# A first sweep whose engine order is worked out in the source: wide ranks, turned tails, decay of two pairs on TensorE

## The chip, the cores and the metric

The kernel runs on one core of one Trainium2 chip. The metric is the device time of the whole program in microseconds (us), as the median of several executions; one execution was also taken by the hardware profiler, and all rows below come from that one.

## The reference

Eight batches of 576 tokens go through eight attention heads of width 64, then a low-rank mixing over tokens, then a two-layer dense net.

```python
scores = q @ k.T / 8                     # per batch and head, 576 x 576
cum    = cumsum(log(clip(f, 1e-4, 1)))   # decay along the sequence
scores = where(causal, -1e9, scores + cum[:, None] - cum[None, :])
x      = softmax(scores) @ v             # heads side by side: 576 x 512
u      = x + ((x.T @ U) @ V).T           # U 576 x 32, V 32 x 576
out    = u + relu(u @ w1) @ w2           # w1 512 x 2048, w2 2048 x 512
```

All is float32. The term `cum[:, None]` is the same along a row and drops out of the softmax.

## The kernel before

Products are done on TensorE in a one-pass format (`F32R`) with each operand split in a high and a low part, three matmuls for one product (high x high, low x high, high x low). The first six pairs of heads use plain float32 scores instead (`terms`, line 291).

**Three stages.** The *first sweep* goes over 32 pairs of heads (four pairs to a batch). For each pair it does attention; for each batch it then does the ranks (`x.T @ U`), the mixing, and the first 6 of 16 chunks of the hidden width of the dense net. It writes `u` and the partial sums to device memory (`ud`, `accd`). A *hand-over* (from line 887) mixes the last batch and does its share of the dense net, while the weights of the other ten chunks are loaded and decoded. The *second sweep* (from line 1075) does those ten chunks for all batches; the change leaves it alone but for the name of one tile.

**A pair of heads.** The 576 rows are four row blocks of 128 and a tail of 64. The scores of a row block i for both heads (`score`, line 297) are matmuls on 64 rows of the array each, into two PSUM banks; `run_a` does blocks 3, 1 and 0, `run_b` block 2 and the tail. For each block, VectorE adds the masked decay and takes the maximum (line 315), and ScalarE takes the exponential (line 324). `turn_p` (line 395) transposes the result on TensorE into a T bank, from where ScalarE or VectorE copies it to `PT` (lines 389, 391). `turn_tail` and `turn_keys` do it for the tail: the last one transposes 64 columns alone (128 x 64). `values` (line 436) multiplies with v, `turn_x` (line 453) transposes back and scales with the reciprocal sums from `inverse` (line 378), `turn_last` does so for the tail, again as a transpose of 64 columns. `split_x` (line 471) makes the high and low parts, and `ranks` (line 485) multiplies them with U, once for each pair, 128 columns wide.

**Decay and masks.** The cumulated decay of all heads is worked out once, written to `cumd` in device memory (line 684) and loaded back for each pair, broadcast over the partitions (`load_decay`, `load_tail`, two buffers each). GpSimd makes the masks from it (`mask`, line 156). Pair 0 doesn't wait for that: TensorE adds its decay with a second matmul, whose weights `picks` hold -8 in the row of the pair's head (line 307).

**Weights.** 14 pieces of the weights (`UNITS`) are loaded as 64-bit numbers and decoded to float32 by six steps (`decode_steps`, line 58): one on ScalarE, four of VectorE's instructions (lines 75, 76, 79, 80), an addition on GpSimd (line 84), a cast on ScalarE (line 85) and a subtraction on GpSimd (line 86). All 14 are decoded within the first seven pairs.

**Dense work.** `ffn_units` (line 577) lists the dense work of a batch as units: six for the first layer of each group of tokens (`l1`, twelve matmuls, tile `A`) and three for each tile of 128 tokens of the second layer (`l2`, six matmuls each, tile `B`). An even batch has 24 units, an odd one 27.

**The order.** `step(t)` (line 720) writes out one pair in ten slots by hand: what TensorE does in each slot, what is put off by how many slots (`defer`), which masks, loads and decodes go where. Dense units are filled in at some slots; `HELD = 4` units of a batch stay over. In the first five steps there is no dense work, and a matmul on `busy` stands in most slots to keep TensorE active (`stay_awake`, line 650). In those steps all engines run in the order of the source (`manual_schedule(engines=None)`); later TensorE, the DMA queue (SP) and GpSimd do, while the compiler's scheduler orders VectorE and ScalarE.

```python
with tc.manual_schedule(engines=None):
    for t in range(EARLY):
        step(t)
with tc.manual_schedule(engines={ET.PE, ET.SP, ET.Pool}):
    for t in range(EARLY, LAST + 1):
        step(t)
```

PSUM has eight banks: four for scores (S), two for transposes and values (T), two for mixing and dense work (F).

Of the kernel before, what the change touches and what calls it, by code (L numbers as in the profile page):

```python
# [8 lines left out]
F32 = mybir.dt.float32  # L9
# [10 lines left out]
DM = H * D  # L20
# [17 lines left out]
NF = 6  # L38


@with_exitstack
def tile_decay_attention_moe(ctx, tc, qk, v, f, U, V, w1, w2, out):
# [56 lines left out]
    sf2 = pool("sf2", 2)  # L99
# [5 lines left out]
    sb2 = pool("sb2", 2)  # L105
    sb3 = pool("sb3", 3)
    psF = ctx.enter_context(tc.tile_pool(name="psF", bufs=2, space=PSUM))
    psS = banks.enter_context(tc.tile_pool(name="psS", bufs=4, space=PSUM))
    psT = banks.enter_context(tc.tile_pool(name="psT", bufs=2, space=PSUM))
# [6 lines left out]
    warm = att.tile([P, 512], BF16, name="warm")  # L116
# [4 lines left out]
    for vr in VR:  # L121
        nc.gpsimd.memset(vr[64:128, NM], 0.0)
    PT4 = att.tile([P, P], F32, name="PT4")
    nc.gpsimd.memset(PT4[64:128], 0.0)
# [3 lines left out]

    def load_decay(p):
        if p >= NP:  # L130
            return
        z = st.setdefault(p, {"M": {}})
        z["decay"] = sb2.tile([P, 2, MAIN], F32, tag="decay", name=f"decay{p}")
        m = z["M"][NM] = sb2.tile([P, S], F32, tag="Mt", name=f"M{p}_t")
        if p == 0:
            nc.gpsimd.memset(z["decay"], 0.0)
            nc.gpsimd.memset(m, 0.0)
            return
        src = cumd.rearrange("(j p) s -> p j s", j=2)[p, :, 0:MAIN]
        nc.sync.dma_start(z["decay"], src.unsqueeze(0).broadcast_to([P, 2, MAIN]))  # L140

    def load_tail(p):
        if not 0 < p < NP:
            return
        m = st[p]["M"][NM]
        for j in range(2):
            nc.sync.dma_start(m[OWN[j]], cumd[j * B * NHP + p].unsqueeze(0).broadcast_to([64, S]))

    def mask(p, i):
        if p >= NP:  # L150
            return
        z = st[p]
        if i < NM:
            w = P * (i + 1)
            m = z["M"][i] = sb.tile([P, 2, w], F32, tag=f"M{i}", name=f"M{p}_{i}")
            nc.gpsimd.affine_select(  # L156
                m, z["decay"][:, :, 0:w], [[0, 2], [-1, w]], ALU.is_ge, MASKED, base=P * i, channel_multiplier=1
            )
            return
        for j in range(2):  # L160
            d = z["M"][NM][OWN[j], MAIN:S]
            nc.gpsimd.affine_select(d, d, [[-1, TAIL]], ALU.is_ge, MASKED, base=0, channel_multiplier=1)
# [24 lines left out]
    staged = {}  # L187

    def load_w(u):
        if u in staged or u >= len(UNITS):  # L190
            return
        kind, fc = UNITS[u]
        n = {"U": (NM + 1) * RK, "V": S}.get(kind, 512)
        if kind == "w2":

            spare = xn[NX - 1].rearrange("p c d -> p (c d)").bitcast(I32)
            if fc % 2:
                raw, a = spare[:, 1536:2560], sb.tile([P, 512], I32, tag="w2a", name=f"stg{u}")
            else:
                raw, a = spare[:, 0:1024], spare[:, 1024:1536]  # L200
        else:
            t = sf.tile([P, 3 * S], I32, tag=("uh", "ul", "hh", "hl")[u % 4], name=f"stg{u}")
            raw, a = t[:, 0 : 2 * n], t[:, 2 * n : 3 * n]
        staged[u] = raw.rearrange("p (n t) -> p n t", t=2), a
        if kind == "w1":
            nc.sync.dma_start(raw, w1_src(fc))
        elif kind == "w2":
            nc.sync.dma_start(raw, w2_src(fc))
        elif kind == "V":
            for g in range(4):  # L210
                nc.sync.dma_start(raw[32 * g : 32 * g + 32], words(V))
        else:
            r4 = raw.rearrange("p (c r) -> p c r", c=NM + 1)
            nc.sync.dma_start(r4[:, 0:NM], words(U[0:MAIN]).rearrange("(c p) r -> p c r", p=P))
            for g in range(2):
                nc.sync.dma_start(r4[64 * g : 64 * g + 64, NM], words(U[MAIN:S]))

    def decode_w(u, spread=None):
        load_w(u)
        raw, a = staged.pop(u)  # L220
        staged[u] = None
        kind, fc = UNITS[u]
        if kind == "w1":
            h, l = (x[:, fc].rearrange("p c f -> p (c f)") for x in (w1h, w1l))
        elif kind == "w2":
            h, l = w2h[:, fc], w2l[:, fc]
        elif kind == "V":
            h, l = VV, VV
        else:
            raw = raw.rearrange("p (c r) t -> p c r t", c=NM + 1)  # L230
            a = a.rearrange("p (c r) -> p c r", c=NM + 1)
            h, l = Us[:, :, 0:RK], Us[:, :, RK : 2 * RK]
        steps = decode_steps(raw, a, h, l, nc.scalar, slice(96, 128) if kind == "V" else slice(0, 128), keep=spread is None)
        if spread:
            for fn, (slots, phase) in zip(steps, spread):
                if slots:
                    defer(phase, fn, slots)
                else:
                    fn()
            return  # L240
        for fn in steps:
            fn()
        if u == len(UNITS) - 1:
            nc.gpsimd.memset(xn[NX - 1][64:128, NM, :], 0.0)


    st = {}
    filler = []

    later = {}  # L250
    now = [0]

    def defer(phase, fn, slots=1):
        later.setdefault(now[0] + slots, []).append((phase, fn))

    def run_later():
        now[0] += 1
        for _, fn in sorted(later.pop(now[0], []), key=lambda x: x[0]):
            fn()

    def run_filler():
        w, fn = filler.pop(0)
        fn()
        return w

    def load_qk(p):

        if p >= NP:
            return
        b, hp = divmod(p, NHP)  # L270
        raw = RAW[p % 2]
        st.setdefault(p, {"M": {}}).update(b=b, hp=hp, raw=raw)
        nc.sync.dma_start(raw[:, KO:QW], qk[p, :, 1])
        nc.sync.dma_start(raw[:, 0:MAIN], qk[p, :, 0, 0:MAIN])
        for j in range(2):
            nc.sync.dma_start(raw[OWN[j], QT + 64 * j : QT + 64 * j + 64], qk[p, OWN[j], 0, MAIN:S])

    def split_qk(p):
        z = st[p]
        z["hi"] = sb.tile([P, QW], F32R, tag="qkh", name=f"qkh{p}")  # L280
        z["lo"] = sb.tile([P, QW], F32R, tag="qkl", name=f"qkl{p}")
        split(z["hi"], z["lo"], z["raw"], nc.scalar, nc.gpsimd)

    def load_v(p):

        vr = VR[p % 2]
        st[p]["vr"] = vr.rearrange("p c (j d) -> p c j d", j=2)
        nc.sync.dma_start(vr[:, 0:NM], v[p, 0:MAIN].rearrange("(c p) d -> p c d", p=P))
        nc.sync.dma_start(vr[0:64, NM], v[p, MAIN:S])

    def terms(p):
        z = st[p]
        if p < NF:
            return ((z["raw"], z["raw"]),)
        return ((z["hi"], z["hi"]), (z["lo"], z["hi"]), (z["hi"], z["lo"]))
# [1197 lines left out]
```

## Time and profile before

| | |
|---|---|
| median of 3 executions | 1247.96 us (1247.14 to 1250.01) |
| the profiled execution, own time | 1248.86 us |
| its span, first to last instruction | 1247.1 us |
| mean granted clock of TensorE | 0.98 |
| the last matmul of the sweep's last ranks | 724.7 us of the span |
| the hand-over ends, second sweep begins | 776.8 us |

The time of an execution is the span and 1.8 us around it. PE is TensorE's matmul unit, PEld its weight loads (beside the matmuls), DVE VectorE, ACT ScalarE, POOL GpSimd, SP the engine whose queue issues nearly all DMAs. Matmuls are pipelined: the row of a matmul shows how long it was under way, so what one costs in a sequence is the distance between starts. A granted clock of 1.00 is TensorE's full level (2.4 GHz), 0.5 its lower one (1.2 GHz).

### The profile page before, as it was taken

The page shows a single profiled execution, that of the slowest core. Times are in us where ns is not written, and L with a number is a line of the kernel's source. Part 1 is how long each engine was busy: PE and PEld are TensorE (multiplying, and loading weights), DVE is VectorE, ACT ScalarE, POOL GpSimd, SP SyncE. Part 2 cuts the span into 40 slices and gives each one's busy share as a digit, 9 for nine tenths or more (in the row PEclk, how much of TensorE's full clock was granted, in tenths as well). Part 3 has the DMA queues.
Part 4 walks back from the last instruction along what each step waited for, and adds up shares of the span by engine and source line. Part 5 has one row for each costly group of instructions (what it writes and reads, how often), then busy time and mean ns, then how long its engine had stood idle before and what let it go on. Part 6 is the DMA issues. An engine that isn't in the chain of part 4 may idle for free.

```text
span 1247.1 us, 23786 instructions
## 1 busy us (share of the span) xinstructions
PE 1178.3 (94%) x8484; PEld 1007.9 (81%) x8489; DVE 841.9 (68%) x2151; ACT 638.2 (51%) x1675; POOL 300.4 (24%) x420
## 2 busy tenths in 40 slices
PE   7777799999999999999998999999999999999998
PEld 4445677886786886878777888878899999999998
DVE  6668856556556556556557679858778687786765
ACT  4565455554555545546536433344555655555553
POOL 4654744333343423434324100000000000000000
PEclk8998899999999999999999999999999999999999
DMA  7544432543535425336325355965775664745533
GB/s 216 152 143 132 126 108 77 163 107 84 150 101 171 120 58 180 103 76 186 109 68 176 119 186 171 336 209 190 236 234 165 208 203 159 256 159 189 191 113 105
DMA packets 124984, 194.36 MB, mean 156 GB/s; under 512 B 16001, under 2 KB 58241, under 8 KB 122817
## 3 DMA queue, kind: packets, MB, share of 16 engines
q1 hardware_dynamic: 124592, 192.57, 49.8%
q8 instruction: 67, 1.10, 0.4%
q14 instruction: 53, 0.43, 0.1%
q10 hardware_dynamic: 272, 0.26, 0.1%
HBM read 145.46 MB, written 47.33 MB: 155 GB/s over the span
## 4 chain that ended last, share of the span: by engine, by line
PE 77%; DVE 10%; issue 3%; DMA 3%; ACT 3%; POOL 3%; SPq 0%; POOLq 0%; ACTq 0%; DVEq 0%
PE pf L1133 15%; PE A L599 12%; PE B L617 10%; PE po L1225 8%; PE V L445 6%; PE T L404 4%; PE px L1225 4%; PE pf L1225 2%; PE Hb L956 2%; PE S_0c L303 2%; PE po L1240 2%; PE O L972 2%; DVE PT L391 2%; PE S_0b L303 1%; PE S_0t L351 1%
## 5 line engine op out<-in xcount | busy, mean ns | idle before, releaser
L1356 ACT COPY mc<-pf 128x512 f32<-128x512 f32 x139 | 81.6, 587 | 168.8 <-PE pf L1133 168.8
L1284 POOL TENSOR_TENSOR xn<-xn,xn 128x512 f32<-128x512 f32 x1 | 1.3, 1267 | 529.5 <-DMA out_dram<-xn 529.5
L404 PE MATMUL T<-ident,P 128*128 128x128 f32 x640 | 103.0, 282 | 24.7 <-ACT PT L389 8.8
L156 POOL TENSOR_SCALAR_AFFINE_SELECT M<-decay 128x1024 f32<-128x1024 f32 (+3 forms) x128 | 94.9, 761 | 119.4 <-DVE nm L315 89.2
L599 PE MATMUL A<-uh,w1h 128*128 128x256 f32 (+1 forms) x384 | 120.8, 315 | 1.0 <-DVE hl L603 0.6
L599 PE MATMUL A<-ul,w1h 128*128 128x256 f32 (+1 forms) x384 | 114.2, 297 | 0.0
L404 PEld LDWEIGHTS T<-ident,P 128*128 128x128 f32 x640 | 77.1, 144 | 45.6 <-ACT PT L389 11.1
L599 PE MATMUL A<-uh,w1l 128*128 128x256 f32 (+1 forms) x384 | 113.9, 297 | 0.0
L176 POOL TENSOR_TENSOR qkl<-raw,qkh 128x1216 fp32r<-128x1216 f32 x26 | 73.1, 2813 | 167.6 <-ACT qkh L173 150.7
L391 DVE COPY PT<-T 128x256 f32<-128x256 f32 (+1 forms) x192 | 73.4, 417 | 44.4 <-PE T L404 43.9
L617 PE MATMUL B<-w2h,hh 128*128 128x512 f32 x216 | 91.4, 423 | 3.4 <-DVE ost L631 3.4
L445 PE MATMUL V<-PT,vr 128*64 128x448 f32 (+3 forms) x640 | 92.0, 435 | 1.5 <-ACT PT L389 1.5
L617 PE MATMUL B<-w2l,hh 128*128 128x512 f32 x216 | 85.1, 394 | 0.0
L617 PE MATMUL B<-w2h,hl 128*128 128x512 f32 x216 | 84.8, 393 | 0.0
L607 ACT ACTIVATE hh<-A 128x256 fp32r<-128x256 f32 (+1 forms) x96 | 39.6, 413 | 86.5 <-PE A L599 86.4
L445 PEld LDWEIGHTS V<-PT,vr 128*64 128x64 f32 x640 | 41.7, 139 | 48.4 <-issue 35.3
L599 PEld LDWEIGHTS A<-uh,w1h 128*128 128x128 f32 x384 | 73.2, 191 | 3.4 <-DVE hl L603 0.8
L603 DVE SCALAR_TENSOR_TENSOR hl<-A,hh 128x256 fp32r<-128x256 f32 (+1 forms) x96 | 43.3, 451 | 45.1 <-ACT hh L607 45.0
L599 PEld LDWEIGHTS A<-uh,w1l 128*128 128x128 f32 x384 | 73.5, 191 | 0.1
L599 PEld LDWEIGHTS A<-ul,w1h 128*128 128x128 f32 x384 | 73.2, 191 | 0.1
L1133 PE MATMUL pf<-d,b1h 128*128 128x256 f32 x320 | 69.6, 280 | 1.3 <-DVE fd L961 1.3
L1137 DVE TENSOR_TENSOR fd<-xn,fd 128x256 fp32r<-128x256 f32 x70 | 38.9, 556 | 34.6 <-ACT fd L1177 32.1
(329 smaller groups left out, 3819.7 us busy)
## 6 DMA issues: line engine op xcount, KB each, us to landing
un<-ud SPq DMA_DIRECT2D x16, 1024.0 KB, 6.4
decay<-cumd SPq DMA_DIRECT2D x31, 512.0 KB, 6.4
d<-ud SPq DMA_DIRECT2D x48, 256.0 KB, 3.8
twd<-xn SPq DMA_DIRECT2D x40, 256.0 KB, 2.9
raw<-in_qk_dram SPq DMA_DIRECT2D x32, 288.0 KB, 6.4
Th<-twd SPq DMA_DIRECT2D x35, 256.0 KB, 3.6
tw<-twd SPq DMA_DIRECT2D x35, 256.0 KB, 2.8
Tl<-twd SPq DMA_DIRECT2D x35, 256.0 KB, 3.2
```

What stands on the lines that cost most here:

```text
L156: nc.gpsimd.affine_select(m, z["decay"][:, :, 0:w], [[0, 2], [-1, w]], ALU.is_ge, MASKED, base=P * i, channel_multiplier=1)
L176: leng.tensor_tensor(dl, src, dh.bitcast(F32), op=ALU.subtract)
L391: defer(2, lambda: nc.vector.tensor_copy(dst, src))
L404: nc.tensor.transpose(tp[:, P * (x + c) : P * (x + c) + P], z["P"][j][i][:, P * c : P * c + P], ident)
L445: nc.tensor.matmul(ps, vr[:, c, j], pt[:, j, c, lo:hi], start=c == 0, stop=lo == 0)
L599: nc.tensor.matmul(ps[:, :nt], wt[:, fc, c], ut[:, c, sl], start=m == 0, stop=m == 3 * NDC - 1)
L603: nc.vector.scalar_tensor_tensor(hl[:, fc, :nt], ps[:, :nt], 0.0, hh.bitcast(F32)[:, fc, :nt], op0=ALU.max, op1=ALU.subtract)
L607: defer(3, lambda: nc.scalar.activation(hh[:, fc, :nt], ps[:, :nt], AF.Relu))
L617: nc.tensor.matmul(ps, ht[:, fc, P * x : P * x + P], wt[:, fc], start=fc == 0 and m == 0, stop=fc == NA - 1 and m == 2,)
L1133: nc.tensor.matmul(ps, a[x][:, c], b[y][:, c], start=start and m == 0, stop=m == 5, skip_group_check=True)
L1225: nc.tensor.matmul(ps[:, HT * x : HT * x + HT], f[a][:, P * x : P * x + P], w[b], start=k.i == 0 and m == 0 and x == 0 and not (k.n == NG ...
L1356: nc.scalar.copy(mc, FA)
```

## The change

All of the first sweep is now described as operations, each with what it reads and writes (keys), its engine or engines with a planned duration, a rank `pr`, and the PSUM banks that it opens and uses. `run()` takes them one after the other: for each engine it finds the operations whose inputs are there (by planned times), takes among those that could start first the one of the lowest rank, and of the engines the one that starts earliest. That gives an order for all five engines, which is then fixed.

```diff
+TURN = 0.08
+AHD = 1.2
+LATE = 2.5
+DEEP = 3.0
+DUE = [0.3, 0.9, 1.5, 2.1, 2.7, 3.3, 3.9, 4.4, 4.8, 5.0, 5.2, 5.5, 5.8, 6.1]
...
+    HOMES = {"S": (0, 1, 2, 3), "T": (4, 5), "F": (6, 7)}
+    LAG = {"PE": 0.23, "DVE": 0.17, "ACT": 0.17, "POOL": 0.12, "SP": 0.06}
+    SLACK = {"PE": 0.25, "DVE": 0.1, "ACT": 0.1, "POOL": 0.1, "SP": 0.0}
...
+    def copy(n, dst, src):
+        return [("ACT", 0.133 + 0.00068 * n, lambda: nc.scalar.copy(dst(), src())), ("DVE", 0.064 + 0.00104 * n, lambda: nc.vector.tensor_copy(dst(), src()))]
+
+    def load(pr, nbytes, fn, r=(), w=()):
+        return op([("SP", 0.45, fn)], pr, r, w, lands=nbytes / 200e3)
...
+    def run():
...
+                        est = max(now, o.ready)
...
+                            if kind == "T" and not state["dense"]:
+                                allowed = (4, 5, 7)
...
+                        if e == "SP":
+                            est = max(est, state["pipe"] - DEEP)
+                        if e == "PE" and o.mode != state["mode"]:
+                            est += 0.15
+                            pr += TURN
+                        cand.append((est, pr, o.n, o, dur, fn, homes))
...
+                first = max(now, min(c[0] for c in cand)) + SLACK[e]
+                c = min((c for c in cand if c[0] <= first), key=lambda c: (c[1], c[2]))
+                if best is None or c[0] < best[0]:
+                    best = (c[0], e, c)
...
+            if e == "PE":
+                if not state["dense"]:
+                    for _ in range(int((est - clock["PE"] - 0.15) / 0.24)):
+                        keep_awake()
...
+        for p in range(NP):
+            b, hp = divmod(p, NHP)
+            inputs(p)
+            scores(p, [(3, 0)], p)
+            scores(p, [(1, 0), (0, 2 * P)], p + 0.1)
+            scores(p, [(2, 0)], p + 0.2)
+            score_tail(p, p + 0.3)
+            for g in range(3):
+                for j in range(2):
+                    turn_p(p, j, g, p + 0.4 + 0.1 * g)
+            turn_tail(p, p + 0.75)
+            inverse(p, p + 0.8)
+            values(p, p + 0.9)
+            turn_x(p, p + 1.05)
+            split_x(p, p + 1.3)
+            if hp == NHP - 1:
+                ranks(b, p + 1.6)
+                if b < B - 1:
+                    mix(b, p + 1.8)
+                    dense(b, p + LATE, 4.0)
+            if p == NP - 4:
+                for i in range(AHEAD):
+                    ahead(i, p + 2.0 + 0.6 * i)
+        run()
```

- *Order.* `step`, its slots, `defer` and the spreading of dense units are gone. PSUM copies (`copy`), the first and the fifth decode step and the subtractions of the low halves of decode and x may go to either of two engines. Scores are three items and a tail for each pair, each of which can be placed by itself. Tiles are allocated once; decay and tail mask have one buffer instead of two.
- *Wide ranks.* `xh` and `xl` hold a whole batch (512 columns), and `ranks` runs once a batch:

```diff
+                    nc.tensor.matmul(bank[0:64], Us[:, i], xx[:, i], start=i == 0 and x == 0, stop=i == NM)
```

- *Turned tails.* The tail's transposes take the last 128 columns, so that the tail arrives on partitions 64 to 127; `PT4`, the tail of v and the reciprocal sums moved there with it:

```diff
+        op([("PE", 0.12, lambda: nc.tensor.transpose(last[:, 0:P], Ptl[:, S - P : S], ident))], pr, [("ptl", 1)], [(last, 0)], opens=[last], mode="F")
+        op(copy(P, lambda: PT4[64:128], lambda: last[64:128, 0:P]), pr + 0.05, [(last, 0)], [("PT4",)], uses=[last])
```

- *Decay of two pairs on TensorE* (`NPK = 2`): pair 1 has `picks` of its own and uses pair 0's masks, which hold no decay; loads of decay and tail mask begin with pair 2.
- *Staying awake.* In place of `busy` matmuls of 512 columns at fixed slots, two of 256 columns stand for each 0.24 us that the plan finds TensorE idle before the first dense work.
- *Hand-over.* No dense units are held over from the batch before the last; the mixing and the dense work of the last batch use all eight banks in turn (`ROUND`).

## Rows read from the trace of the kernel before

**Rows 1.** The page: engine totals, 40 slices of TensorE, its granted clock.

```profile
PE 1178.3 (94%) x8484; PEld 1007.9 (81%) x8489; DVE 841.9 (68%) x2151; ACT 638.2 (51%) x1675; POOL 300.4 (24%) x420
...
PE   7777799999999999999998999999999999999998
...
PEclk8998899999999999999999999999999999999999
```

**Rows 2.** Windows of the front: length, busy us of each engine, clock, DMA share, GB/s.

```profile
6.70:26.20 19.50, 13.56 (x74) 8.15 (x74) 14.73 (x36) 9.30 (x29) 8.50 (x11) 0.86 0.85 238
...
6.70:99.90 93.20, 72.59 (x426) 45.39 (x430) 63.87 (x189) 50.73 (x150) 49.50 (x67) 0.87 0.56 160
99.90:157.10 57.20, 43.46 (x288) 32.32 (x287) 46.66 (x104) 27.97 (x78) 33.66 (x33) 0.88 0.47 139
```

**Rows 3.** Windows of five batches, of the sweep's end, of the hand-over.

```profile
178.80:617.70 438.90, 422.78 (x3116) 342.74 (x3115) 252.81 (x775) 224.10 (x647) 168.29 (x240) 1.00 0.42 121
617.70:724.70 107.00, 100.33 (x718) 80.81 (x717) 68.88 (x190) 50.80 (x143) 29.59 (x42) 0.98 0.34 113
724.70:776.80 52.10, 51.08 (x287) 45.45 (x285) 48.03 (x103) 22.60 (x48) 0.00 (x0) 1.00 0.59 201
```

**Rows 4.** The chain of waits from 6 to 46 us: start, us, what.

```profile
8.51 3.26 DMA cumd<-fl
11.79 6.53 DMA decay<-cumd
...
27.35 4.23 issue
...
38.09 4.16 issue
```

**Rows 5.** GpSimd in order of time: start, us, instruction, idle before, releaser.

```profile
31.59 0.18 POOL L385 COPY rv<-rv 64x1 f32<-64x1 f32 x1 [4.25 <-DVE rv L384]
...
42.29 1.34 POOL L479 TENSOR_TENSOR xl<-xn,xh 128x512 fp32r<-128x512 f32 x1 [4.20 <-ACT xh L478]
```

**Rows 6.** One window for tile A, then for tile B (columns as above, without GpSimd).

```profile
99.90:157.10 57.20, 10.01 (x72) 8.95 (x72) 2.44 (x6) 2.34 (x6) 0.88 0.47 139
...
99.90:157.10 57.20, 3.28 (x12) 2.11 (x12) 0.00 (x0) 0.88 0.47 139
```

**Rows 7.** TensorE's waits, 178.8 to 617.7: total us, times, longest.

```profile
PE Tu L546 <- DVE ul L537: 4.3, 10, 0.6
...
PE T L404 <- DVE PT L391: 2.3, 6, 0.5
```

**Rows 8.** TensorE in order of time, where scores follow dense work.

```profile
698.92 0.40 PE L617 MATMUL B<-w2h,hl 128*128 128x512 f32 x1
699.15 0.40 PE L617 MATMUL B<-w2l,hh 128*128 128x512 f32 x1
699.48 0.44 PE L303 MATMUL S_0b<-qkh 64*128 64x384 f32 x1
```

**Rows 9.** TensorE in order of time, around a narrow transpose.

```profile
713.68 0.60 PE L413 MATMUL T_t<-ident,Ptl 128*128 128x128 f32 x4
714.12 0.27 PE L418 MATMUL Ty<-ident,Ptl 128*64 128x128 f32 x1
714.15 0.36 PE L599 MATMUL A<-uh,w1h 128*128 128x256 f32 x1
714.35 0.28 PE L599 MATMUL A<-uh,w1l 128*128 128x256 f32 x1
714.47 0.28 PE L599 MATMUL A<-ul,w1h 128*128 128x256 f32 x1
```

**Rows 10.** One decode step on VectorE: ns min/median/max, first and last start.

```profile
L79 DVE TENSOR_SCALAR sr<-xn x16: 411/420/424, 728.7 to 822.1; 128x512 int32<-128x512 int32 x16
...
L79 DVE TENSOR_SCALAR xn<-stg x3: 413/1391/2915, 117.6 to 150.5; 128x512 int32<-128x512 int32 x3
```

More of the change, by code (lines that the diff above doesn't have):

```diff
@@ new lines, in tile_decay_attention_moe, with __init__, __getitem__ @@
+    FB_ = [psF.tile([P, 512], F32, tag="F", name=f"F{x}") for x in range(2)]
+    busy = FB_[0]
+    still = ident.bitcast(BF16)
+    NP = B * NHP
+    cur = [UH, UL]
+    late_a = Late(lambda: sb.tile([P, 512], I32, tag="w2a", name="w2a"))
+    class Bank:
+        def __init__(self, kind):
+            self.kind, self.left, self.home, self.at = kind, 0, None, 0.0
+        def __getitem__(self, k):
+            return SPACE[self.home][k]
+    SPACE = SB_ + TB_ + FB_
+    HOMES = {"S": (0, 1, 2, 3), "T": (4, 5), "F": (6, 7)}
@@ new lines, in tile_decay_attention_moe, with dense, l1, go @@
+    made = [0]
+    def dense(b, pr, span):
+        x = xn[b % NX]
+        units, sizes = [], []
+        for t0, nt in ((0, 256), (256, 256)) if b % 2 == 0 else ((0, 256), (256, 384)):
+            chunks = (0, 1) if t0 == 0 else (2, 3) if nt == 256 else (2, 3, 4, 5)
+            def l1(fc, pr, t0=t0, nt=nt, chunks=chunks):
+                bank = Bank("F")
+                sl = slice(t0, t0 + nt)
+                def go():
+                    m = 0
+                    for c in range(NDC):
+                        for wt, ut in ((w1h, UH), (w1l, UH), (w1h, UL)):
+                            nc.tensor.matmul(bank[:, :nt], wt[:, fc, c], ut[:, c, sl], start=m == 0, stop=m == 3 * NDC - 1)
+                            m += 1
@@ new lines, in l2 @@
+                op([("DVE", 1.2, two)], pr, [(bank, 0)] + X(b, NM) + X(b - 1, NM), [("ost", k)], uses=[bank])
+                load(pr + 0.2, 262e3, lambda: nc.sync.dma_start(accd[B, b // 2], ost), r=[("ost", k)])
+            units += [(nt * 12 * 0.00046, l1, fc) for fc in range(NA)]
+            units += [(6 * 0.231, l2, (part, y)) for y in ((2, 0, 1) if nt > 2 * P else (0, 1)) for part in range(NA // 2)]
+        total, gone, out_ = sum(u[0] for u in units), 0.0, []
+        for d, fn, k in units:
+            at = len(todo)
+            fn(k, pr + span * gone / total)
+            gone += d
+            out_.append(todo[at:])
@@ new lines, in tile_decay_attention_moe @@
+        known(5.6, *(("M", i) for i in range(NM)), ("Mt", 0), ("Mt", 1))
+        clock.update(PE=6.3, DVE=7.5, ACT=5.4, POOL=6.6, SP=2.7)
+        state["pipe"] = 6.0
+        load(0.0, 147e3, lambda: nc.sync.dma_start(cumd, fl[0 : B * H]), r=[("fl",)] + [("xl", h) for h in range(NHP)], w=[("cumd",)])
+        for p in range(1, NPK):
+            op([("DVE", 1.5, lambda p=p: [pick(p, x) for x in range(4)])], p - 0.6, [("warm",)], [("picks", p)])
+        for u in range(len(UNITS)):
+            weights(u)
```

1107 lines of the change are left out of this document (542 added, 565 removed).

## The prediction, made before the change was run

> **What bounds the kernel now.** I read the page's engine totals and slices first, then the windows by stage and by batch, then the chain of waits where TensorE is idle. The page shows TensorE busy 1178.3 of 1247.1 us [rows 1]: whatever the change does, it can win back little more than the idle 69 us, the time at the lower clock, and work that is inflated by waits. The slices show where that is: the first five or six read 7 or 8 tenths at a granted clock of 0.8 to 0.9, the rest read 9 [rows 1]. The windows say it in us [rows 2]. From 6.7 to 99.9, five pairs of heads take 93.2 us, 18.6 us each, and no engine is full: TensorE 72.59 (with the stay-awake matmuls in it), VectorE 63.87, ScalarE 50.73, GpSimd 49.50. The next two pairs take 57.2 us with TensorE at 43.46. From 178.8 to 617.7 it is another regime: five batches in 438.9 us, 87.8 each, with TensorE busy 422.78 [rows 3]. So the sweep has two stages: a front that is bound by the order of small steps on several engines, and a long part that is bound by TensorE.
>
> What the front waits for is seen in the chain: the write of the cumulated decay takes 3.26 us, its reload as the broadcast decay of pair 1 another 6.53, and two pieces of over 4 us each are "issue" [rows 4]. GpSimd's rows tell what those two are: a 0.18 us copy that sat 4.25 us until the reciprocal came from VectorE, and the low half of x that sat 4.20 us until ScalarE had cast the high half [rows 5]. GpSimd runs in program order, so its masks and decode steps stood behind those two instructions. That is an order that costs, not an engine that is full.
>
> **The change, part by part.** The times are of the profiled execution: span 1247.1, own time 1248.86, which is 0.9 above the median 1247.96.
>
> *Pair 1's decay on TensorE, and the planned order in the front.* Pair 1 no longer needs the written and reloaded decay (3.26 + 6.53 us and four masks behind them); it pays one more set of `picks` matmuls and four small VectorE instructions (the existing ones are off the trace's long waits, and TensorE has 20 of 93 us free there, so I price them at nothing; without that cover they are a few us). What then sets the pace of a pair? Engine work per pair today is 63.87/5 = 12.8 on VectorE, 50.73/5 = 10.1 on ScalarE, 9.9 on GpSimd [rows 2]. The new order may give each PSUM copy to either of the first two, so (12.8 + 10.1)/2 = 11.5 us is the floor of an even share. Transfers: 160 GB/s over 93.2 us are 14.9 MB, 3.0 MB a pair; at the 238 GB/s of the first step [rows 2] that is 12.5 us, at the 200 GB/s for which the new order plans its loads 15 us. Decay and tail mask have one buffer now instead of two, so a load stands behind the last mask of the pair before. I take 15 us a pair, the slow end. By the priorities the dense layer of batch 0 starts between pair 5 and 6. Pair 5's middle is then reached at 6.7 + 5.5 x 15 = 89. From there each pair carries its share of dense work (24 units a batch, six a pair) and runs at the pace of the long part, 87.8/4 = 21.9 us [rows 3]: the remaining 1.5 pairs take 32.9 and bring along nine dense units, where the kernel before has done eight by 157.1 (72 matmuls of twelve a unit, 12 of six) [rows 6]. So the state of 157.1 is reached at 122: **35 us less**. Bounds: at 12.5 us a pair 49 less; if only the reload at pair 1 goes, 10 less. I take 35 because its slow terms, transfers and steady pace, are both measured.
>
> *The long part.* TensorE's work stays: same columns in scores, values, dense. Idle is 438.9 - 422.8 = 16.1 us, 3.2 a batch [rows 3], in some seven stops, each of half a microsecond and mostly behind VectorE [rows 7] (two of nine kinds of them stand there). Each stop also costs a refill of about 0.16 (a transpose lasts 0.27 by itself, and follows the one before by 0.11 when nothing stops [rows 9]), so 4.3 us a batch hang on order. An order picked by readiness should remove some 60%, 2.6. Against it, scores are now three items a pair, not two runs, and a run of 64-row score matmuls starts 0.33 behind the last dense matmul, where the dense matmuls follow each other by 0.23 [rows 8]: 0.1 us for an entry, and I take as much for leaving it. If half of the pairs get a third entry, that is 0.4 a batch. Net 2.2 x 5 = **11 us less**. Bounds: 22 less (all of the 4.3 goes), 10 more (an entry more for every pair, and none of the idle back but half as much again). At the end of the sweep, 617.7 to 724.7, TensorE is idle 6.7 of 107 us [rows 3]; I take **3 less**.
>
> *Wide ranks.* Nine matmuls of 512 columns replace 36 of 128: the same columns, so nothing on TensorE; fewer copies on ScalarE and VectorE, which are not full. They wait for the batch's last pair, as the mixing did before.
>
> *Turned tails.* The two narrow transposes a pair (128 x 64) become full ones. Do the narrow ones cost anything? Four tail transposes start at 713.68, the narrow one follows at 714.12, that is 4 x 0.11; the dense matmul behind it starts 0.03 later and the next one 0.20 after that: 0.23 for both, where 0.11 + 0.12 is what they cost in a plain sequence [rows 9]. So by the rows the narrow transpose is free and I price the change at 0. If each paid 0.1 us going in and coming out, as the scores do, the change would give 4 x 0.1 x 32 = 13 us: one of the rivals. The Trainium skill, TensorEngine Tiling (Array Packing), section Key Properties, says that changing the tiling mode drains TensorE; by that rule those 13 us would be there, rows 9 show none of them, and the entry into 64-row scores in rows 8 agrees with it.
>
> *The hand-over.* The sweep left four dense units for the stage behind it; now it does them itself, 4 x 6 x 0.23 = 5.5 us, and the mixing of the last batch has no such filler between its steps. That stage would be as much shorter on TensorE, but its VectorE is busy 48.03 of 52.1 us with the next weights [rows 3], so it hardly shortens: **4 us more** (0 to 5.5).
>
> Sum: -35 - 11 - 3 + 4 = -45; 1248.9 - 45 = 1203.9, and 0.9 off to the median: **1203 us**.
>
> **The rivals.**
> *Slower: late evacuations at two banks.* The order is worked out from planned durations and then fixed on every engine. A pair turns some twelve T banks, of which only two exist once dense work runs, and TensorE, in order, stops wherever the copy before is late. Break-even is 45 us / 26 pairs / 12 = 0.14 us for each turn. At 0.25 us each it is 78 us: 1203 + 78 = 1281. For it: today's stops are of this kind, and one at a PT copy lasts up to 0.5 us [rows 7]. Against it: those are six in 20 pairs, copies are now taken by whichever of two engines is free, and dense work is a filler at every turn. Chance 0.11.
>
> *The front is held by VectorE behind GpSimd.* The same decode step takes 0.42 us when GpSimd is idle and between 0.41 and 2.92, median 1.39, for three between 117 and 151 us when GpSimd works beside it [rows 10]. The new order has no such price in it and packs the 14 weight decodes beside masks and GpSimd's share. If two of the four steps of each decode lose 0.65 us, VectorE has 18 us more in the front, and if that is its longest engine, 35 becomes 17: 1221. The Trainium skill, SBUF — State Buffer, section Who interferes with whom, says that the two engines share one pair of ports and that the later one blocks for the whole instruction, which agrees with these rows. Chance of this kind of half gain (1212 to 1238): 0.27.
>
> *The long part gains all its idle, or the front runs at 12.5 us a pair, or the narrow transposes did cost:* -22, or -49, or -13 in place of their terms: 1178 to 1192. Chance 0.19.
>
> *The front gains only pair 1's reload, and the long part nothing:* -10 + 4: about 1242, still faster by 0.5%. Chance 0.05.
>
> *The change doesn't do what it says:* an engine's order is still decided by the longest wait, and both stages stay. Within 0.2%, which is about what a measurement of this kernel can tell from no change: 0.03.
>
> **How the numbers follow.** Forecast as worked out, 1192 to 1212: 0.35. With 0.27 + 0.19 + 0.05 that is faster by over 0.2%: 0.86; same 0.03; slower 0.11. The predicted time is the likeliest, 1203. The range 1178 to 1240 takes in the bounds of front and long part; it leaves out the slower case and what is left of the others, some 0.18.
>
> **What would show it.** Right: first wide ranks and steady dense matmuls from 80 to 95 us on; slices two to five of TensorE at 8 or 9 and a clock of 0.9 or more; VectorE's share in the first 90 us above 75%; the sweep ends (last ranks) near 685 where it ends at 724.7 now; the stage behind the sweep still about 52 us, with TensorE waiting on VectorE's weight steps. Wrong: steady batches over 88 us, with TensorE's waits on PT copies grown past 5 us a batch (the slower case); decode steps of over 1 us all through the front (VectorE behind GpSimd); pairs 1 to 4 still 18 us apart with GpSimd or SP waiting in order (the plan does not hold on the chip).

## The result, and the profile after

The changed kernel takes 1203.39 us where the kernel before took 1247.55 in the same series: 0.9647 of it, interval 0.9621 to 0.9673. One execution of that series, the profiled one, took 3905.5 us in a disturbed state, so the profile after is that of a second series of the same kernel: 1198.91 us (1195.82 to 1201.52) beside 1248.56, 0.9604 (0.9580 to 0.9627), profiled execution 1196.7, span 1194.9. The times below stand against this span and the 1247.1 of before.

From the page of the changed kernel: TensorE's total, then the slices of TensorE, VectorE and the granted clock.

```profile
PE 1158.4 (97%) x8292; PEld 992.8 (83%) x8292; DVE 860.9 (72%) x2131; ACT 636.7 (53%) x1684; POOL 277.4 (23%) x409
...
PE   9888999999999999999999898999999999999997
...
DVE  8998666576665666665588799658768778687765
...
PEclk9998999999999999999999999999999999999999
```

The first slices of TensorE read 8 and 9 where they read 7 [rows 1], with one clock digit of 8 left, and VectorE's read 8 and 9.

To put stages side by side I cut both traces where the ranks of a batch's last pair start: batch 0, 1, 6 and 7 at 97.4, 195.9, 639.2 and 723.5 before, at 74.1, 164.6, 589.0 and 664.3 after. At the later three marks nearly as many dense units are done in both (12 units of the first kind and 7 of the second before, 12 and 8 after; 72 and 76 in both; 84 and 89, 84 and 88). So a difference between marks is one in speed, but for one unit of the second kind: six matmuls at 0.23, 1.4 us. The front does it earlier, the long part has it less, and the end of the sweep leaves one more to the hand-over. Windows of the kernel before between these marks, and from the last ranks on (length, busy us of TensorE, its loads, VectorE, ScalarE, GpSimd; clock, DMA share, GB/s):

```profile
97.40:195.90 98.50, 83.39 (x575) 64.37 (x574) 68.55 (x176) 49.37 (x141) 55.04 (x65) 0.90 0.41 118
195.90:639.20 443.30, 427.47 (x3121) 346.33 (x3121) 254.73 (x777) 224.26 (x645) 169.22 (x245) 1.00 0.42 119
639.20:723.50 84.30, 78.26 (x571) 62.83 (x570) 55.89 (x153) 40.67 (x113) 21.35 (x31) 0.98 0.39 129
...
777.00:826.10 49.10, 47.55 (x198) 37.63 (x197) 40.42 (x80) 16.46 (x30) 0.00 (x0) 0.97 0.80 279
826.10:1247.10 421.00, 414.10 (x3314) 405.33 (x3312) 306.94 (x668) 232.26 (x549) 1.27 (x1) 1.00 0.58 187
```

The same for the changed kernel, with the first five pairs (6.7 to 75.0) and the stretch behind them ahead:

```profile
6.70:75.00 68.30, 62.21 (x403) 38.99 (x402) 65.19 (x186) 48.56 (x149) 29.37 (x44) 1.00 0.63 181
75.00:99.90 24.90, 18.57 (x112) 11.59 (x110) 24.03 (x50) 13.16 (x33) 17.00 (x19) 0.93 0.61 188
74.10:164.60 90.50, 79.92 (x553) 61.78 (x553) 71.29 (x181) 51.92 (x147) 51.58 (x65) 0.94 0.50 143
164.60:589.00 424.40, 420.79 (x2985) 340.69 (x2984) 265.13 (x761) 226.23 (x657) 162.30 (x248) 1.00 0.46 126
589.00:664.30 75.30, 74.79 (x537) 59.12 (x536) 58.92 (x150) 37.23 (x106) 26.61 (x36) 1.00 0.40 137
666.60:713.30 46.70, 43.28 (x248) 38.66 (x248) 43.00 (x92) 21.12 (x44) 0.00 (x0) 1.00 0.63 213
713.30:773.10 59.80, 55.95 (x233) 44.62 (x232) 47.90 (x93) 19.30 (x36) 0.00 (x0) 0.97 0.81 279
773.10:1194.90 421.80, 414.81 (x3320) 406.01 (x3318) 306.01 (x666) 231.78 (x547) 1.27 (x1) 1.00 0.55 181
```

| Stage | before | after | difference | predicted |
|---|---|---|---|---|
| start to the ranks of batch 1 | 195.9 | 164.6 | -31.3 | -35 |
| to the ranks of batch 6 (five batches) | 443.3 | 424.4 | -18.9 | -11 |
| to the ranks of batch 7 | 84.3 | 75.3 | -9.0 | -3 |
| the last ranks themselves | 1.4 | 2.3 | +0.9 | 0 |
| behind them, to the end | 522.2 | 528.3 | +6.1 | +4 |

**Front.** Five pairs take 68.3 us, 13.7 each, where they took 18.6 [rows 2]. VectorE is busy 65.19 of these, 95%, and TensorE 62.21. What VectorE waited for in these 68 us (us in total, times, longest):

```profile
DVE fr L885 <- ACT fl L883: 0.7, 1, 0.7
DVE rv L590 <- POOL sm L587: 0.4, 1, 0.4
DVE S L529 <- ACT P L535: 0.3, 1, 0.3
DVE w1l L391 <- ACT w1h L395: 0.3, 1, 0.3
```

That is 1.7 us. So these pairs are now bound by one full engine, and no longer by order or by transfers. Behind them, from 75.0 to 99.9, VectorE is busy 24.03 of 24.9: batch 0's mixing and the decode of the w2 pieces stand there together, and the next pair's tail exponentials end 30.7 us behind those of the fifth (105.8 after 75.1). From 99.9 to batch 1's ranks VectorE is full no more: what is left of its windows is 46.4 of 64.7 us.

**Long part.** TensorE is idle 3.6 of 424.4 us, where it was idle 15.8 of 443.3, and 6.7 us less busy. Its waits there now (columns as in [rows 7]):

```profile
PE F L733 <- DVE ul L726: 1.2, 2, 0.6
PE S L552 <- ACT P L535: 0.9, 1, 0.9
PE F L733 <- DVE xn L718: 0.5, 2, 0.2
```

Counted from TensorE's matmuls in order of time, it stops 20 times there instead of 41. Its turns between scores, values and the rest are 136 instead of 118 if the tail's scores are counted in. But those are matmuls on all 128 rows, and they hardly cost a turn (the first four lines); the values (the last two) do cost one:

```profile
224.16 0.34 PE L779 MATMUL F<-ul,w1h 128*128 128x384 f32 x1
224.33 0.30 PE L552 MATMUL S<-qkh 128*128 128x288 f32 x1
...
202.97 0.30 PE L552 MATMUL S<-qkl,qkh 128*128 128x288 f32 x1
203.10 0.40 PE L800 MATMUL F<-w2h,hh 128*128 128x512 f32 x1
...
213.89 0.39 PE L800 MATMUL F<-w2l,hh 128*128 128x512 f32 x1
214.21 0.33 PE L639 MATMUL T<-PT,vr 128*64 128x128 f32 x2
```

A tail score starts 0.17 behind a dense matmul of 384 columns, as the next dense one does, and a dense matmul starts 0.13 behind a tail score, as the next tail score does. The values start 0.32 behind a dense matmul of 512 columns, where the next dense one would start after 0.23. Counted by what costs something, matmuls on 64 rows, values and the rest, the turns are 122 instead of 128.

**Behind the sweep.** TensorE's busy time is the same within 1.3 us (43.28 + 55.95 + 414.81 = 514.0; before 512.7), which fits the one dense unit more (1.4). The other 4.8 of the +6.1 are idle.

### The profile page after: what moved, and what is told of

Read it like the earlier page. It is cut to its first block, busy times and chain, and to the rows that moved or that the text cites. A ratio compares the mean times of both kernels' runs of the same rounds, so it can differ in the third digit from the quotient of the medians.

```text
span 3903.7 us, 23433 instructions
## 1 busy us (share of the span) xinstructions
PE 3896.9 (100%) x8292; PEld 2810.1 (72%) x8292; DVE 882.6 (23%) x2131; ACT 648.7 (17%) x1684; POOL 271.2 (7%) x409
## 4 chain that ended last, share of the span: by engine, by line
PE 100%; DVE 0%; issue 0%
PE pf L1232 18%; PE F L779 12%; PE F L800 12%; PE po L1324 9%; PE T L639 8%; PE T L602 6%; PE S L511 6%; PE px L1324 4%; PE O L1071 3%; PE Hb L1055 3%; PE po L1339 3%; PE S L552 2%; PE pf L1324 2%; PE T L703 1%; PE T L658 1%; PE T L621 1%
## 5 line engine op out<-in xcount | busy, mean ns | idle before, releaser
L639 PE MATMUL T<-PT,vr 128*64 128x448 f32 (+2 forms) x632 | 317.7, 1261 | 0.0
L602 PE MATMUL T<-ident,P 128*128 128x128 f32 x610 | 273.5, 669 | 0.0
L779 PE MATMUL F<-uh,w1h 128*128 128x256 f32 (+1 forms) x348 | 271.0, 779 | 0.0
L779 PE MATMUL F<-uh,w1l 128*128 128x256 f32 (+1 forms) x348 | 254.1, 730 | 0.0
L779 PE MATMUL F<-ul,w1h 128*128 128x256 f32 (+1 forms) x348 | 251.6, 723 | 0.0
L800 PE MATMUL F<-w2h,hh 128*128 128x512 f32 x192 | 229.0, 1192 | 0.0
L800 PE MATMUL F<-w2h,hl 128*128 128x512 f32 x192 | 211.3, 1101 | 0.0
L800 PE MATMUL F<-w2l,hh 128*128 128x512 f32 x192 | 209.9, 1093 | 0.0
L779 PEld LDWEIGHTS F<-ul,w1h 128*128 128x128 f32 x348 | 173.0, 497 | 13.9 <-issue 9.7
L779 PEld LDWEIGHTS F<-uh,w1l 128*128 128x128 f32 x348 | 171.2, 492 | 13.8 <-issue 10.8
```

Source lines behind the costliest of these rows:

```text
L602: nc.tensor.transpose(bank[:, P * x : P * x + P], PP[i][j][:, P * c : P * c + P], ident)
L639: nc.tensor.matmul(ps, vr[:, c, j], PT[:, j, c, lo:hi], start=c == 0, stop=lo == 0)
L779: nc.tensor.matmul(bank[:, :nt], wt[:, fc, c], ut[:, c, sl], start=m == 0, stop=m == 3 * NDC - 1)
L800: nc.tensor.matmul(bank[:, :], ht[:, fc, P * y : P * y + P], wt[:, fc], start=fc == 0 and m == 0, stop=fc == NA - 1 and m == 2,)
```

## The experiments

Each kernel below is the changed kernel with one edit, timed beside the kernel before on its chip. Two kernels of different series are compared by their ratios.

**The same kernel again**

> The changed kernel as it is, for an undisturbed profile. My theory: 1203 us; the state that the kernel before reaches at 157.1 us is reached near 122, five batches of the long part take 428 us in place of 438.9, the hand-over still about 52 us with TensorE waiting on VectorE's weight steps. Rival (VectorE held by GpSimd in the front): the front gains under 20 us, decode steps of over 1 us all through it, and the long part gains 25 or more.

Measured: 0.9604 (0.9580 to 0.9627), the profile shown above. That differs from the first series by 0.4%, so chips or series differ by as much: edits of different series that lie under 5 us apart are not told apart. The twelve runs of this section were taken in series of four, in the order in which they stand. The start of batch 1's ranks scatters by itself: the run below that moves the next weights' subtractions to GpSimd has the same instructions in the same order up to there, and there they start at 167.4 instead of 164.6, while its five batches take 424.6 instead of 424.4. An edit in the first sweep also makes the planner choose another order, so a few us of a difference can be the order and not the edit.

**Pair 1's decay by reload**

```diff
-NPK = 2
+NPK = 1
```

> Pair 1 loads its decay again (one number: NPK 1 in place of 2), all else as changed. My theory: the planned order gives the front its gain and pair 1's reload is worth 5 to 10 us of it: 1208 to 1213 us. Rival (the reload is what the front waited for): 20 us or more are lost, 1223 us or more. Rival (the plan hides the reload behind other work): under 2 us lost.

Measured: 1201.32 us, 0.9627 (0.9605 to 0.9648). The tail exponentials of pair 1 end at 37.8 instead of 35.0, and batch 1's ranks start at 166.4 instead of 164.6, less than the mark's scatter. The reload that stood at the head of the chain of before [rows 4] is worth some 2 us at most once the order is planned, not the 5 to 10 that I expected.

**Narrow tails**

```diff
-nc.tensor.transpose(last[:, 0:P], Ptl[:, S - P : S], ident)
+nc.tensor.transpose(last[0:64, 0:P], Ptl[:, MAIN:S], ident)
...
-nc.tensor.transpose(last[:, 0:P], xT[:, S - P : S], ident)
+nc.tensor.transpose(last[0:64, 0:P], xT[:, MAIN:S], ident)
```

(and the buffers behind them back to partitions 0 to 63)

> The tails' transposes are 64 columns again (two a pair), all else as changed. My theory: a narrow transpose costs what a full one costs, so 1203 us within 3. Rival (a change of the tiling mode drains TensorE, 0.1 us in and out): 13 us more, 1216 us.

Measured: 1193.68 us, 0.9569 (0.9542 to 0.9595); the interval overlaps that of the changed kernel. TensorE in order of time around the same transpose, first in the changed kernel (wide), then with the edit (narrow); start, us, instruction:

```profile
304.19 0.66 PE L658 MATMUL T<-ident,xT 128*128 128x128 f32 x4
304.68 0.27 PE L678 MATMUL T<-ident,xT 128*128 128x128 f32 x1
304.71 0.48 PE L800 MATMUL F<-w2h,hh 128*128 128x512 f32 x1
305.03 0.39 PE L800 MATMUL F<-w2h,hl 128*128 128x512 f32 x1
```

```profile
301.95 0.66 PE L658 MATMUL T<-ident,xT 128*128 128x128 f32 x4
302.44 0.27 PE L678 MATMUL T<-ident,xT 128*64 128x128 f32 x1
302.47 0.47 PE L800 MATMUL F<-w2h,hh 128*128 128x512 f32 x1
302.78 0.39 PE L800 MATMUL F<-w2h,hl 128*128 128x512 f32 x1
```

Wide: 0.49, 0.03, 0.32 from start to start. Narrow: 0.49, 0.03, 0.31. A transpose into 64 columns costs what one into 128 does, and turning the tails won nothing. The Trainium skill, TensorEngine Tiling (Array Packing), section Key Properties, says that a change of tiling mode drains TensorE; these rows show no drain for a transpose into 64 output columns. It is not the 64 columns as such: the values have the same form (128*64) and start 0.09 later than a dense matmul would (0.32 for 0.23, the rows above). What sets the two apart is not shown.

**Ranks once a pair**

```diff
-ranks(b, p + 1.6)            # once a batch, 512 columns
+ranks(p, p + 1.6)            # every pair, 128 columns
```

> Ranks once a pair and 128 columns wide again, all else as changed. My theory: the columns are the same, so nothing on TensorE but three more small groups a batch: 1203 us, at most 4 more. Rival (each of the 24 extra groups stops TensorE twice for 0.1 us and its three copies delay others): 8 us more or above, 1211 us.

Measured: 1200.48 us, 0.9614 (0.9593 to 0.9634); five batches take 425.6 instead of 424.4, with TensorE busy 420.45 where it was 420.79. The wide ranks are worth 1 to 2 us at most, and none of it in TensorE's busy time.

**The next weights' subtractions on GpSimd, behind the sweep**

```diff
-decode(t.rearrange(...), a, h, l, nc.scalar, sub=nc.vector)
+decode(t.rearrange(...), a, h, l, nc.scalar, sub=nc.gpsimd)
```

> In the hand-over and behind it the addition and the subtraction of each of the 16 weight decodes go to GpSimd, which is idle there; VectorE loses 32 instructions of 0.68 us. Theory (VectorE holds the hand-over: 713 to 773 us there took 60 us where the kernel before took 49): the ten first chunks of the second sweep take about 50 us, the whole 8 to 12 us less than the changed kernel, ratio to the kernel before about 0.952. Rival (GpSimd's 1.3 us steps and its share of the ports make the chain as long): within 3 us of the changed kernel, ratio 0.960.

Measured: 1210.74 us, 0.9684 (0.9668 to 0.9700), some 10 us slower than without the edit: my theory and the rival both missed. One line of VectorE's weight sums (additions and subtractions) in the changed kernel, then with the edit (ns min/median/max, first and last start):

```profile
L973 DVE TENSOR_TENSOR xn<-xn x10: 415/420/425, 680.0 to 752.9; 128x256 f32<-128x256 f32 x10
```

```profile
L973 DVE TENSOR_TENSOR xn<-xn x10: 411/1505/1522, 682.1 to 749.3; 128x256 f32<-128x256 f32 x10
```

TensorE's longest wait in that stage, again in the changed kernel and then with the edit:

```profile
PE Hb L1055 <- DVE xn L811: 3.8, 1, 3.8
```

```profile
PE Hb L1055 <- DVE xn L811: 10.2, 1, 10.2
```

GpSimd took 32 additions and subtractions of 0.68 us off VectorE, and in the 118 us behind the ranks VectorE is still busy 92.92 where it was 94.77, with 39 instructions fewer: what was taken away came back as longer instructions. The 0.42 us weight sum takes 1.51 beside GpSimd's additions of 1.59 us and subtractions of 1.39 to 1.41 (means). The Trainium skill, SBUF — State Buffer, section Who interferes with whom, says that a VectorE instruction with two inputs in SBUF contends with a GpSimd instruction that reads SBUF, by an exclusive lock. These rows agree that they contend; the time added is 1.1 us, less than one whole GpSimd instruction.

**The sweep's subtractions on GpSimd alone**

```diff
-[("POOL", 0.1 + 1.13 * k, ...), ("DVE", 0.06 + 0.54 * k, ...)]
+[("POOL", 0.1 + 1.13 * k, ...)]          # also x's low part and its rows
```

> In the sweep the additions and subtractions of decode and of x's low half may go to GpSimd alone; VectorE, 95% busy from 6.7 to 75 us, loses some 10 us of work in the front. Theory (VectorE's amount of work sets the front): the ranks of batch 1 start 5 to 8 us earlier than at 164.6. Rival (the chain of a decode and the ports count, GpSimd takes 1.3 us where VectorE takes 0.69): not earlier, or up to 5 us later.

Measured: 1192.00 us, 0.9536 (0.9521 to 0.9550): faster than the changed kernel, the intervals apart. Batch 1's ranks start at 157.0 instead of 164.6, which is about the whole gain, and 6.5 of these 7.6 us are there when the tail exponentials of pair 5 end (99.3 instead of 105.8). VectorE's busy time from 6.7 us to batch 1's ranks falls from 64.33 + 71.29 = 135.6 to 59.75 + 70.13 = 129.9 us (two windows each). So 5.7 us off VectorE come with 7.6 us off the time: its load moves the front, and here the move to GpSimd pays, where behind the sweep it doesn't. The 1.9 us more are within the scatter of this mark.

**Copies on the engines of before**

```diff
-op(copy(...), ...)
+op(copy(...)[:1], ...)       # or [1:], as the kernel before had it
```

> Every PSUM copy has the engine that it had in the kernel before, no choice; the order is planned as in the change. Theory (the choice between two engines carries much of the front's gain, since VectorE is its longest engine): ranks of batch 1 8 to 15 us later than 164.6, the long part within 5 us of its 424.4, the whole some 1210 us. Rival (the order alone carries it): within 3 us everywhere.

Measured: 1196.72 us, 0.9575 (0.9560 to 0.9589). My expectation missed: that a copy may go to either engine, which stood in my floor of 11.5 us a pair, carries none of the gain here. Batch 1's ranks even start at 160.3, 4.3 us earlier, though VectorE is as busy up to them (136.1 us for 135.6). So the order that the planner finds, with the scatter of the mark, moves it by 4 us with VectorE's load unchanged.

**No stay-awake matmuls**

```diff
-keep_awake()
+pass
```

> No stay-awake matmuls after the first twelve. Theory (TensorE is busy 91% of the front with real work): the granted clock falls for at most a few us, the ranks of batch 1 within 3 us of 164.6. Rival (the front's gain rests on the clock, 0.87 before and 1.00 after from 6.7 to 75): clock under 0.9 there and ranks of batch 1 10 us later or more.

Measured: 1198.99 us, 0.9591 (0.9577 to 0.9606). Batch 1's ranks start at 166.1, within the scatter. The clock granted from 6.7 to 75 is 0.98 instead of 1.00, from 75 to 130 it is 0.88 instead of 0.91; the time is the same. So the front's clock and gain hardly hang on these matmuls.

**The two gains together**

> Two edits that each gained alone are put together: the sweep's decode adds, low parts of the weights and of x, and gathered rows on GpSimd alone (0.9536 of the kernel before), and the last key chunk's transposes 64 columns wide on partitions 0 to 63 (0.9569), where the changed kernel stood at 0.9604. If the two gains are separate (the front is VectorE's; the tails gain something else) they add: 0.950, some 1187 us, batch 1's ranks at 156 or before, and 665 us from the start to the end of the last ranks falls to 656. If the narrow tails' gain was only a run's scatter, the time stays at that of the first edit alone, 1190 to 1193.

Measured: **1188.18 us, 0.9518 (0.9501 to 0.9535)**, the fastest kernel of this study, 0.9% below the changed kernel. Batch 1's ranks start at 156.1; its windows to there and over the five batches:

```profile
70.90:156.10 85.20, 77.09 (x541) 61.28 (x539) 67.38 (x172) 47.89 (x139) 58.27 (x71) 0.94 0.50 151
156.10:577.00 420.90, 418.23 (x2985) 340.28 (x2984) 249.51 (x740) 226.59 (x659) 173.22 (x266) 1.00 0.47 127
```

The five batches take 3.5 us less than in the changed kernel, 2.6 of it in TensorE's busy time. What the narrow tails save there the rows do not tell: a single transpose costs the same. Whether their gain is one at all stays open: the time lies between the 1187 of the two added and the 1190 of the first alone, and its interval overlaps that of the first edit (0.9521 to 0.9550).

**All three together**

> As the run before, and every copy out of PSUM fixed to the engine that made it in the kernel before (alone 0.9575). If the fixed copies help by taking VectorE's turns out of the front, they add to the tails but not to the subtractions, which freed VectorE already: 1185 to 1191 us. If the free choice matters once VectorE has room, it is 2 to 4 us slower than the run before.

Measured: 1194.48 us, 0.9567 (0.9552 to 0.9582), slower than the run before. Beside the subtractions on GpSimd, the free choice of the copying engine is worth 6 us, more than I gave it. Only 2.6 of it are there at batch 1's ranks (158.7 for 156.1), so that it is worth this because VectorE was relieved in the front is not shown.

**A plan that believes in early results**

```diff
-LAG = {"PE": 0.23, "DVE": 0.17, "ACT": 0.17, "POOL": 0.12, "SP": 0.06}
+LAG = {"PE": 0.0, "DVE": 0.0, "ACT": 0.0, "POOL": 0.0, "SP": 0.0}
...
-return [("ACT", 0.133 + 0.00068 * n, ...), ("DVE", 0.064 + 0.00104 * n, ...)]
+return [("ACT", 0.066 + 0.00034 * n, ...), ("DVE", 0.032 + 0.00052 * n, ...)]
```

> The planner believes that a result can be used at once (no lag behind any engine) and that a copy out of PSUM costs half; the work is the same, only its picked order differs. The rival of late evacuations: TensorE's order then runs ahead of the copies at the two T banks, each batch of the long part stops for it (88 us a batch and more, over 20 us slower, above 1215 us), with waits of TensorE on the copies of the transposes that together make over 10 us from batch 1's ranks to batch 6's. My theory, that the dense units between give each copy time enough and the exact prices matter little: that stretch stays at 424 to 428 us, its waits under 5 us, the time at 1197 to 1204 us.

Measured: **1258.49 us, 1.0078 (1.0062 to 1.0094)**: slower than the kernel before, though the work is that of the changed kernel; order differs, and with it the engine of some copies and the number of stay-awake matmuls. My expectation fell, the rival's held. Five batches with this plan, and TensorE's longest waits in them:

```profile
174.70:630.00 455.30, 430.39 (x2988) 340.15 (x2986) 272.13 (x765) 221.99 (x648) 166.17 (x251) 1.00 0.43 117
```

```profile
PE T L602 <- ACT PT L258: 11.7, 21, 1.0
PE S L552 <- ACT P L535: 3.0, 7, 0.5
...
PE F L733 <- DVE ul L726: 2.9, 8, 0.5
PE T L602 <- DVE PT L258: 2.1, 3, 0.7
```

TensorE stops 61 times instead of 20 and is idle 24.9 us instead of 3.6, over half of it where a transpose waits for the PT copy that holds its bank. With 41 stops more it is also busy 9.6 us longer, 0.23 a stop to fill up again, or 0.3 if its 17 turns fewer (105) saved the 0.16 each that the next run shows. Single stops of the changed kernel between two transposes give 0.22: the last transpose shows 0.27 where the next one else starts 0.11 behind it, and the first one after the stop is followed after 0.17 instead of 0.11. The end of the sweep (630.0 to 719.6) takes 89.6 us instead of 75.3, and batch 1's ranks come 10 us later. The plan's prices are not an ornament: its lags and copy durations, which this run changed together, carry more than the whole gain.

**A plan with free turns**

```diff
-TURN = 0.08
+TURN = 0.0
...
-                            est += 0.15
+                            est += 0.0
...
-                    for _ in range(int((est - clock["PE"] - 0.15) / 0.24)):
+                    for _ in range(int((est - clock["PE"]) / 0.24)):
```

(The last line lets the planner put a few more stay-awake matmuls in the front.)

> The planner sees no price in a switch of TensorE between the scores, the values and the rest (its 0.15 us and the rank penalty are 0); again only the order differs. If TensorE's busy time in the long part fell from 427.7 to 421.0 us because the order groups the kinds, the switches come back with it: 425 us or more busy there, 1200 to 1206 us. If the busy time fell for another reason (no instruction fetch between the batches, the entries of the score chunks as they are), it stays at 420 to 422 us and the time within 2 us of 1199.

Measured: 1197.02 us, 0.9581 (0.9566 to 0.9596). Its window of the five batches:

```profile
163.00:591.50 428.50, 425.40 (x2985) 339.01 (x2984) 264.92 (x754) 229.16 (x660) 162.71 (x249) 1.00 0.44 125
```

TensorE turns 151 times there instead of 122 (tail scores not counted) and is busy 4.6 us longer, 0.16 a turn, as the first theory had it; but its time, 1200 to 1206, was not met: the front is 1.6 us shorter, which is within its scatter, and the stage behind the sweep 2.9. So a turn has its price, and the total does not show 4 us of it.

**What the runs say together.** Of the parts that were taken back one by one, the reload, the turned tails, the wide ranks, the free copies and the stay-awake matmuls, none costs more than 2.4 us. The early plan, which keeps all of them, loses more than the whole gain. So the order carries the gain; the single buffers of decay and tail mask and the new hand-over were not run alone.

## Why the prediction was right, and where it wasn't

The time, 1203, was met by the first series to 0.4 us and by the second to 4. Some of that is luck: the terms miss by +3.7, -7.9, -6.0 and +3 us (the last with the ranks' 0.9 in it), and misses of both signs partly cancel.

**Front: -31.3 for -35.** The pace was 13.7 us a pair, not 15, and it was set by another thing. I took the transfers, at 200 GB/s; the rows show VectorE at 95% with 1.7 us of waits beside transfers of 181 GB/s, and the run with the subtractions on GpSimd shows that VectorE's load moves the time. My own number for VectorE was there, 12.8 a pair, but I let the copies be shared with ScalarE, and that sharing carried nothing in the changed kernel. Then the step "from there each pair runs at 21.9" held as a mean alone: by their tail exponentials the next four pairs took 30.7, 23.4, 16.1 and 18.7, 22.2 each. Pair 5 is the long one, as batch 0's mixing and the w2 decodes fall there on the same full engine. The first error gave 5 x 1.3 us back, pair 5 alone took 8.8. The -35 was forecast for the state of 157.1 us, and the mark of the table lies 39 us behind it, so the two are not quite the same stretch.

**Long part: -18.9 for -11.** The mechanism held: an order picked by readiness removes stops. The sizes were off. Idle fell by 12.2 of 15.8 us, 77% and not 60%. A stop's refill is 0.22 and not 0.16, so 21 stops fewer are 4.6 of the 6.7 us that TensorE is busy less. The turns I feared did not come on balance. Runs of 64-row scores did grow, 40 to 46, but values now often stand right beside scores, and the turns that cost fell by 6, 1.0 us at 0.16. The dense unit that the front has already done is 1.4, and six transposes more between these marks cost 0.7. That adds up to 6.3 of 6.7; the wide ranks have no part in it.

**End of the sweep: -9.0 for -3.** Of 6.0 us idle 0.5 are left, and the busy time falls by 3.5, of which 1.4 are the dense unit that is left to the hand-over. I had put 3 of 6.7 there without a reason other than caution; this stretch is of the long part's kind and should have had its share.

**Wide ranks and turned tails: 0 and 0.** Both right within what can be measured; the narrow tails were even a little better, with overlapping intervals. The rival in which narrow transposes cost 13 us is refuted by the rows, as [rows 9] had said.

**Hand-over: +6.1 for +4.** The sign and the cause held in part. The step that failed is "now it does them itself": the planner still leaves five dense units of batch 6 behind the last ranks, one more than before, so TensorE's work there did not shrink; but they now run at once, ahead of the mixing, which then has nothing between its steps: two new waits of 1.8 and 1.5 us. And the last tile's add of the dense result stands behind the weight steps on VectorE: 3.8 us, the row shown above. The first matmul on the next weights comes 46.7 us behind the ranks instead of 52.1, which looks like a gain and is none: 41 matmuls of the old dense work run behind it, where before none did.

**The rivals.** *Late evacuations*: not here, but real. The early plan is that case, and its five batches' 30.9 us more over 20 pairs and twelve turns are 0.13 us a turn, beside the break-even of 0.14 that the prediction worked out; with what it loses at both ends it comes out slower than before. What speaks against it in the changed kernel is only that its plan prices lags and copies well. *VectorE behind GpSimd in the front*: half right. VectorE is the bound, but its steps grew less than in the kernel before, and not by the 18 us of this rival. The decode step of [rows 10] in the front of the changed kernel, up to 165 us:

```profile
L371 DVE TENSOR_SCALAR stg<-stg x8: 248/428/958, 11.8 to 69.1; 128x512 int32<-128x512 int32 x6, 128x160 int32<-128x160 int32 x1, 128x576 int32<-128x576 int32 x1
L371 DVE TENSOR_SCALAR xn<-xn x6: 416/424/1655, 76.8 to 117.5; 128x512 int32<-128x512 int32 x6
```

Medians of 0.43 and 0.42 us, longest 0.96 and 1.66, where some took 1.4 to 2.9. Over all four decode steps, those of 512 columns up to batch 1's ranks are together 6.5 us longer than at 0.42 and 0.69 each (9 of 48 by over 0.2); in the kernel before it is 12.9, and with the subtractions on GpSimd alone 9.0. *Only the reload*: refuted, the reload is the small part (2 us). Of the signs named in advance, TensorE's slices, VectorE's share (84.0 of the first 90 us) and the steady batches (84.9 us each) came as said. The clock did but for one slice of 0.8. The first wide ranks came at 74.1, but dense work began at 97.4 and not from 80 to 95, and the sweep's end at 666.6 came earlier than the 685 expected.

## What to carry to other kernels

When every engine is planned in the source, price the lag from an engine's end to its result's use and the time of each PSUM copy: with those prices halved or gone the same work ran 5% slower than with them. Before costing a re-ordered stage, add up each engine's busy time per tile; the longest of them is the pace that remains, and work taken off that engine is what to try first. Moving VectorE's additions and subtractions to GpSimd paid in the front, where the decode steps left on VectorE grew by 2.5 us, and lost behind the sweep, where some 20 of the 22 us moved came back as longer steps; look at the neighbour's durations, not at the busy time that was moved.

## What the runs showed of the hardware

- Ten weight sums of VectorE (256 columns, two SBUF inputs) went from 0.42 to 1.51 us (median) beside GpSimd's additions and subtractions; the line's other ten, with other operands, stayed at 0.42 in the median, the longest of them 1.53.
- A stop of TensorE between transposes costs the wait and 0.22 us more at the granted clock 1.00 (0.27 for 0.11, 0.17 for 0.11). Over five batches the early plan gives 0.23 to 0.3.
- A turn of TensorE into 64-row scores or values costs 0.09 to 0.1 us from start to start (0.32 or 0.33 for 0.23), and 0.16 on average over 29 turns more in five batches. Tail scores on 128 rows hardly cost one (0.17 in, 0.13 out).
- A transpose into 64 output columns starts and ends as one into 128 does (0.49, 0.03 and 0.31 or 0.32).
- The stay-awake matmuls made no difference of time, with the clock from 75 to 130 us granted at 0.88 or 0.91.
